# Block maxima on all partitions, mask zeroing on VectorE, and copies dealt anew among three engines

## The chip, the cores and the metric

The kernel runs on one core of one Trainium2 chip. The metric is the device time of one execution in microseconds (us). TensorE (PE) multiplies, VectorE (DVE), ScalarE (ACT) and GpSimd (POOL) work on tiles, SyncE (SP) issues most of the transfers. A profile is one execution of the program, taken by the hardware profiler. PEld are TensorE's weight loads, and a name with a q behind it (SPq) is an engine's queue of issued transfers.

## What is computed

Three layers follow one another: block-causal attention (blocks of 64), a feed-forward layer with a gated convolution over the sequence, and a feed-forward layer with a spatial gate. Cut to what matters:

```python
# attention: q, k, v of 4 x 8 x 576 x 64
scores = np.matmul(q, k.transpose(0, 1, 3, 2)) / np.sqrt(64)
scores = np.where(block_i >= block_j, scores, -1e9)
scores = scores - np.max(scores, axis=-1, keepdims=True)
attn = np.exp(scores)
attn = attn / (np.sum(attn, axis=-1, keepdims=True) + 1e-09)
x = np.matmul(attn, v)                      # then 4 x 576 x 512
# first layer, d_ff = 1024
h = np.maximum(x @ w_in, 0.0)
conv = sum(conv_w[k] * shift(h, k - 1) for k in range(3))
x = (h * sigmoid(conv)) @ w_out
# second layer
h = np.maximum(x @ w_in, 0.0)
u, v = h[..., :512], h[..., 512:]
v_n = (v - mean(v)) / sqrt(var(v) + 1e-6)
out = (u * (w_spatial @ v_n + b_spatial)) @ w_out
```

## The kernel before

The 32 heads are worked off as 16 pairs; a pair's two heads lie on partitions 0 to 63 and 64 to 127. For each pair the program loads keys and queries (`raw`), rounds both (`kp`, `qp`), and TensorE multiplies them once for the maxima alone (steps x0 to x3 of a pair, `tile_max` and `last_max`). VectorE reduces these scores out of PSUM. A 128-query tile holds two blocks of 64: the lower block sees the keys up to its own block, the upper one 64 keys more. So `mx` takes the maximum over what both see, on 128 partitions, and `mxu` the maximum over the 64 further keys, on partitions 64 to 127 only. The last block of 64 queries, whose queries lie in `qlast` for both heads, has 576 keys; when its scores lie in two banks, two reductions go to `mxl` and are joined. `max_up` joins `mx` and `mxu`, and TensorE transposes the result (`max_tr`). The row of maxima then goes by a transfer into the mask operand `mq`, and a product of `mk` and `mq` subtracts the maximum and masks in the score bank itself (line 1028). ACT takes the exponential, TensorE sums with the values, and `norm_a` normalises.

All products of the two layers run on float32 numbers that are split into a rounded high part and the rest, the low part (`h` and `l` in names), three products for each. The weights come as 64-bit words, and `words_to_f32` makes them float32 in steps (a scaled copy on ACT, a sign mask, two shifts); `split64` then makes high and low part. For each of the 64 gate tiles (`in1`), ACT and VectorE make the convolution and the gate, and GpSimd rounds the result into `g` (line 662); the low part is a subtraction on VectorE or GpSimd (`minus`, line 669).

What runs where is fixed by hand-made tables: `SEQ` is the order of TensorE's steps (x, y: maxima; s: scores; v: value sums; m: first layer; p: second layer; f: matmuls that only fill), `ORDER` the order on each other engine, `BIND` which buffer a step takes. Masks of bits (`KL_POOL`, `SGN_POOL`, `Q_DVE` and so on) say which engine has a copy or a low part. `Order` plays the program through with estimated durations and emits the instructions in that order.

At the start GpSimd zeroes `mk` and three `mq`, and issues the transfers of their constant rows (`start`, lines 1312 to 1317); VectorE zeroes the rest (`start2`), and TensorE spins on 16 small products until the first keys land.

## Time and profile before

| what | value |
|---|---|
| median of 3 runs | 606.75 us (605.97 to 607.78) |
| the profiled execution, its own time | 607.56 us |
| its span, first to last instruction | 605.70 us |
| TensorE busy | 576.7 us, 95% |
| VectorE busy | 443.8 us, 73% |
| ACT busy, GpSimd busy | 249.1 us, 214.1 us |
| TensorE's granted clock, mean | 0.985 |

The shares are means over stages that differ. The attention with its preparations fills roughly the first 140 us, then attention and the first layer run beside one another until about 290 us, the first layer ends near 405 us, and the rest is the second layer. An idle time in a row stands in brackets, with what ended it. Busy shares by stretch tell which engine has no time left in a stretch; idle time of TensorE can be read directly as a stretch's length less its busy time.

### The profile page before, as it was taken

How to read it: one execution, taken by the hardware profiler on the slowest of the kernel's cores; microseconds unless marked ns; L12 is line 12 of the kernel's file. 1: busy time of each engine (PE TensorE's matmuls, PEld its weight loads, DVE VectorE, ACT ScalarE, POOL GpSimd, SP SyncE). 2: the span in 40 equal slices, each digit the busy share in tenths (PEclk: the TensorE clock that was granted, in tenths of full speed). 3: DMA queues.
4: the chain of work that ended last, by engine and by line, in shares of the span. 5: the costliest groups of instructions: out<-in, count | busy, mean ns of one | idle time of the engine just before them, and what ended most of it. 6: DMA issues, size and time to landing. Idle time of an engine off the chain costs nothing.

```text
span 605.7 us, 11928 instructions
## 1 busy us (share of the span) xinstructions
PE 576.7 (95%) x4612; PEld 515.0 (85%) x4612; DVE 443.8 (73%) x930; ACT 249.1 (41%) x517; POOL 214.1 (35%) x269
## 2 busy tenths in 40 slices
PE   6888789999999999999999999999999999999997
PEld 4655467879898888889988999999989989998996
DVE  4999989985919786986835489877797474455556
ACT  3565545554346542534525275636063023013101
POOL 5422423536352556446414354643211121121020
PEclk7999989999999999999999999999999999999999
DMA  7554453015132213303012474434713400520012
GB/s 225 183 187 157 152 177 122 0 60 161 43 99 62 89 53 123 101 21 121 1 41 82 122 237 152 136 109 110 227 37 106 137 31 0 163 74 2 22 38 78
DMA packets 43542, 61.22 MB, mean 101 GB/s; under 512 B 8949, under 2 KB 34293, under 8 KB 43486
## 3 DMA queue, kind: packets, MB, share of 16 engines
q1 hardware_dynamic: 43226, 60.37, 31.1%
q8 instruction: 36, 0.59, 0.4%
q0 software_dynamic: 256, 0.09, 0.1%
q14 instruction: 20, 0.16, 0.1%
q10 hardware_dynamic: 4, 0.00, 0.0%
HBM read 46.08 MB, written 14.23 MB: 100 GB/s over the span
## 4 chain that ended last, share of the span: by engine, by line
PE 62%; DVE 12%; ACT 2%; issue 1%; POOL 1%; DVEq 0%; POOLq 0%; ACTq 0%
PE mo L651 41%; PE s L651 11%; PE st L659 3%; DVE cc L1195 3%; PE st L1024 3%; DVE cc L1199 1%; PE st L651 1%; DVE g L665 1%; DVE mx L903 1%; PE st L1028 1%; PE st L1016 1%; PE st L898 1%; DVE w_f L753 1%; DVE x L665 0%; DVE mxu L903 0%
## 5 line engine op out<-in xcount | busy, mean ns | idle before, releaser
L651 PE MATMUL mo<-x,w1i_h 128*128 128x290 f32 x504 | 108.0, 301 | 1.3 <-ACT h L1189 0.7
L651 PE MATMUL mo<-g,w1o_h 128*128 128x288 f32 x464 | 98.1, 298 | 0.5 <-ACT h L1189 0.5
L651 PEld LDWEIGHTS mo<-x,w1i_h 128*128 128x128 f32 x504 | 82.8, 188 | 5.0 <-issue 1.9
L1195 DVE SCALAR_TENSOR_TENSOR cc<-h,cwt,cc 128x288 f32<-128x288 f32 x128 | 71.1, 573 | 21.0 <-ACT cc L1192 20.3
L651 PEld LDWEIGHTS mo<-g,w1o_h 128*128 128x128 f32 x464 | 76.1, 189 | 2.9 <-issue 1.7
L662 POOL TENSOR_SCALAR g<-cc 128x288 fp32r<-128x288 f32 x64 | 38.9, 612 | 105.3 <-DVE cc L1199 97.4
L651 PE MATMUL mo<-x,w1i_l 128*128 128x290 f32 x252 | 75.0, 297 | 0.0
L651 PE MATMUL mo<-g,w1o_l 128*128 128x288 f32 x232 | 68.6, 296 | 0.0
L1037 ACT ACTIVATE e<-st 128x1024 f32<-128x1024 f32 (+1 forms) x64 | 53.1, 836 | 32.3 <-PE st L1028 26.1
L662 POOL TENSOR_SCALAR g<-ga 128x288 fp32r<-128x288 f32 x40 | 19.4, 496 | 100.3 <-DVE ga L1518 54.3
L651 PE MATMUL mo<-x,w2i_h 128*128 128x288 f32 x256 | 51.8, 295 | 0.1
L659 PE MATMUL st<-e,v 128*64 128x448 f32 (+4 forms) x384 | 49.2, 407 | 0.5 <-DVE mt L966 0.5
L651 PEld LDWEIGHTS mo<-x,w1i_l 128*128 128x128 f32 x252 | 47.4, 188 | 0.0
L659 PEld LDWEIGHTS st<-e,v 128*64 128x64 f32 x384 | 26.0, 142 | 24.7 <-issue 18.0
L903 DVE TENSOR_REDUCE mx<-st 128x2 f32<-128x640 f32 (+2 forms) x64 | 42.5, 679 | 6.1 <-PE st L898 5.8
L651 PEld LDWEIGHTS mo<-g,w1o_l 128*128 128x128 f32 x232 | 43.6, 188 | 0.0
L651 PEld LDWEIGHTS mo<-x,w2i_h 128*128 128x128 f32 x256 | 41.2, 188 | 0.5 <-ACT u L1492 0.3
L1192 ACT ACTIVATE cc<-h,cwt 128x288 f32<-128x288 f32 x64 | 33.9, 534 | 15.7 <-DVE g L665 11.0
L651 PE MATMUL s<-w2i_h,x 128*128 128x512 f32 x128 | 39.5, 390 | 0.0
L651 PE MATMUL mo<-ws_h,vnh 128*128 128x288 f32 x135 | 39.4, 296 | 0.0
L1197 ACT ACTIVATE cc<-cc 128x288 f32<-128x288 f32 x64 | 27.8, 439 | 24.3 <-DVE cc L1195 23.9
L651 PE MATMUL mo<-x,w2i_l 128*128 128x288 f32 x128 | 37.7, 294 | 0.0
(186 smaller groups left out, 1408.6 us busy)
## 6 DMA issues: line engine op xcount, KB each, us to landing
x2d<-y SPq DMA_DIRECT2D x32, 288.0 KB
x<-x2d SPq DMA_DIRECT2D x16, 576.0 KB
raw<-in_kq_dram SPq DMA_DIRECT2D x15, 576.0 KB
v<-in_vt_dram SPq DMA_DIRECT2D x16, 320.0 KB
rb<-rd SPq DMA_DIRECT2D x32, 144.0 KB
out_dram<-o SPq DMA_DIRECT2D x32, 144.0 KB
x<-in_w2i_dram SPq DMA_DIRECT2D x8, 512.0 KB
w_raw<-in_w1i_dram SPq DMA_DIRECT2D x4, 512.0 KB
```

The costliest lines, as they stand in the source:

```text
L651: nc.tensor.matmul(o, w, x, start=start, stop=stop)
L659: nc.tensor.matmul(o[row:row + m], w, x, start=start, stop=stop)
L662: nc.gpsimd.tensor_scalar(o, i, 1.0, 0.0, ALU.mult, ALU.add)
L665: nc.vector.tensor_tensor(o, a, b, ALU.subtract)
L753: yield ("DVE", t_dve(n), lambda: nc.vector.scalar_tensor_tensor(f.bitcast(U32), f.bitcast(U32), 3, s, ALU.logical_shift_left, ALU.bitwise ...
L898: nc.tensor.matmul(st[:, e, o:o + n], qp[r, 128 * c:128 * c + 128], kp[r, 0:n], start=True, stop=True)
L903: return ("DVE", t_dve(2 * i.shape[-1] * (i.shape[2] if len(i.shape) == 4 else 1)), lambda: nc.vector.tensor_reduce(o, i, AX.X, ALU.max), ...
L1024: nc.tensor.matmul(st[:, e, o:o + nq], keys(kx, slice(64 * e, 64 * e + 64)), qx[e], start=j == 0, stop=False)
L1037: yield ("ACT", t_act(2 * n), lambda: nc.scalar.activation(ex[:, :, e0:e0 + n], st[:, :, 0:n], ACTF.Exp, scale=0.125), 0, 0)
L1192: yield ("ACT", t_act(HT, False, 1), lambda: nc.scalar.activation(cc, h[:, o:o + HT], ACTF.Copy, scale=cwt[:, c, 1:2]), 0, P_G)
L1195: yield ("DVE", t_dve(HT, ptr=1), lambda: nc.vector.scalar_tensor_tensor(cc, h[:, o + e:o + e + HT], cwt[:, c, j:j + 1], cc, ALU.mult, ALU ...
L1197: yield ("ACT", t_act(HT, False), lambda: nc.scalar.activation(cc, cc, ACTF.Tanh, scale=0.5), 0, P_G)
```

## The change

- The upper maxima `mxu` are reduced on all 128 partitions. On the lower 64 they then hold something that must not count, so `max_up` joins with a limit per partition: minimum with `lim` (-3.0e38 below, 3.0e38 above), then maximum with `mx`, in one scalar_tensor_tensor. The join of the two halves of the last block becomes a reduction over two elements. The small buffers are four deep instead of two.
- VectorE zeroes `mk` and the three `mq`; GpSimd issues only their transfers. All zeroing is emitted ahead of the first load.
- The bit masks are replaced by `ENG`, a table with a letter for each instance (A, D or P). New are the choices for the high parts of weights (`WH`), of `x` (`XH`) and `g` (`GH`), for each key and query copy (`K`, `Q`), each half of `qlast` (`QE`), and each of the four score sums of a pair (`ADD`).
- `SEQ`, `ORDER` and `BIND` are new tables. Among the first transfers, the convolution's taps (`cwr`) and the identity come earlier, and pair 1 is loaded before pair 2. TensorE's sequence has 26 filling products instead of 32 (the 16 of the spin among them).

```diff
-                    yield red(up[64:128].rearrange("p (e c) -> p e c", e=2)[:, :, 0:2],
-                              st.rearrange("p e (i x) -> p e i x", x=256)[64:128, :, :, 64:128])
+                    yield red(up.rearrange("p (e c) -> p e c", e=2)[:, :, 0:2],
+                              st.rearrange("p e (i x) -> p e i x", x=256)[:, :, :, 64:128])
...
-                    yield red(up[64:128, c:8:4], st[64:128, :, 128 * c + 64:128 * c + 128])
+                    yield red(up[:, c:8:4], st[:, :, 128 * c + 64:128 * c + 128])
...
-                    yield ("DVE", 0.08, lambda: nc.vector.tensor_tensor(mx[:, 8:9], two[:, 0:1], two[:, 1:2], ALU.max), 0, 0, True)
+                    yield ("DVE", 0.09, lambda: nc.vector.tensor_reduce(mx[:, 8:9], two, AX.X, ALU.max), 0, 0)
...
-        yield ("DVE", 0.08, lambda: nc.vector.tensor_tensor(mx[64:128, 0:8], mx[64:128, 0:8], up[64:128], ALU.max), 0, 0, True)
+        yield ("DVE", 0.14, lambda: nc.vector.scalar_tensor_tensor(
+            mx[:, 0:8], up, lim, mx[:, 0:8], ALU.min, ALU.max), 0, 0, True)
...
-        yield ("ACT", t_act(512, False), lambda: nc.scalar.activation(hi, fv, ACTF.Copy), 0, prio)
-        yield minus(not (W_DVE >> unit) & 1, lo, fv, raw(hi), 512, prio)
+        yield copies("WH", unit, hi, fv, 512, prio)
+        yield minus("W", unit, lo, fv, raw(hi), 512, prio)
...
-        yield ("POOL", t_round(S), lambda: pool_round(x1[:, 0, :], x), 0, NPR + 1)
-        yield minus((X1_POOL >> p) & 1, x1[:, 1, :], x, raw(x1[:, 0, :]), S, NPR + 1)
+        yield copies("XH", p, x1[:, 0, :], x, S, NPR + 1)
+        yield minus("X", p, x1[:, 1, :], x, raw(x1[:, 0, :]), S, NPR + 1)
...
-                yield ("POOL", t_round(HT), lambda: pool_round(g[:, 0, :], cc), 0, P_G)
-                yield minus((GLO_POOL[2 * b + hf] >> c) & 1, g[:, 1, :], cc, raw(g[:, 0, :]), HT, P_G)
+                yield copies("GH", 16 * b + 8 * hf + c, g[:, 0, :], cc, HT, P_G)
+                yield minus("G", 16 * b + 8 * hf + c, g[:, 1, :], cc, raw(g[:, 0, :]), HT, P_G)
...
     def start():
-        for t, c in [(mk, 0)] + [(t, 1) for t in mq]:
-            nc.gpsimd.memset(raw(t), 0.0)
-            for e in range(2):
-                nc.gpsimd.dma_start(out=t[64 * e:64 * e + 5], in_=kc[c])
-        yield ("POOL", 6.4, None, 0, 0)
+        yield ("POOL", 1.9, consts([(mk, 0)], nc.gpsimd))
+        yield ("mark", ("mk",))
+        yield ("POOL", 3.2, consts([(t, 1) for t in mq], nc.gpsimd))
...
+    def zeros():
         spin(od_mo[0])
         nc.vector.memset(eps, 1e-6)
+        for t in [mk] + mq:
+            nc.vector.memset(raw(t), 0.0)
+        nc.vector.memset(lim[0:64], -3.0e38)
+        nc.vector.memset(lim[64:128], 3.0e38)
...
+ENG = {
...
+    "WH": "PDAPAPPPPAPDPPDPDPDPPDAP",
+    "K": "APPPPDPPPAAAAPPPP",
+    "GH": "PAPAPAPPDAPDPAPADDAPPAAAPDAPAAAPPDPAPAAPAAAADAAPAAPDAPAAAAAPDPAP",
...
+    def copies(table, i, o, x, n, prio):
+        return alt(table, i,
+                   A=on("A", n, lambda: nc.scalar.activation(o, x, ACTF.Copy), prio),
+                   D=on("D", n, lambda: nc.vector.tensor_copy(o, x), prio, fast=True),
+                   P=on("P", n, lambda: pool_round(o, x), prio))
```

Three places show how instructions move. First GpSimd at the start; `mk` and `mq` are the mask operands, `qlast` the last 64 queries of a pair (a number behind a name counts buffers). Before:

```order
L1314 MEMSET mk 128x576
L1316 DMA mk<-in_kc_dram 5x576 x2
L1314 MEMSET mq_147 128x576
L1316 DMA mq_147<-in_kc_dram 5x576 x2
L1314 MEMSET mq_148 128x576
L1316 DMA mq_148<-in_kc_dram 5x576 x2
L1314 MEMSET mq_149 128x576
L1316 DMA mq_149<-in_kc_dram 5x576 x2
L662 ISA
L662 TENSOR_SCALAR qlast_150<-raw 64x64 x2
```

Now:

```order
L1332 DMA mk<-in_kc_dram 5x576 x2
L666 ISA
L666 TENSOR_SCALAR kp_153<-raw 128x320
L1332 DMA mq_148<-in_kc_dram 5x576 x2
L1332 DMA mq_149<-in_kc_dram 5x576 x2
L1332 DMA mq_150<-in_kc_dram 5x576 x2
L666 TENSOR_SCALAR kp_155<-raw 128x576
L666 TENSOR_SCALAR qlast_152<-raw 64x64
```

Pair 0's `qlast` has left this queue (ACT makes it), the second half of pair 0's keys has come into it, and the zeroing is gone.

Second VectorE during the maxima of pair 3, up to the join (L951 before, L969 now). Before:

```order
L903 TENSOR_REDUCE mxu<-st_111 64x2
L903 TENSOR_REDUCE mx<-st_110 128x2
L941 TENSOR_TENSOR mx<-mxl 128x1
L749 TENSOR_SCALAR x_448<-x_448 128x512
L903 TENSOR_REDUCE mxu<-st_110 64x2x2
L903 TENSOR_REDUCE mx<-st_110 128x2
L751 SCALAR_TENSOR_TENSOR x_448<-x_448 128x512
L824 CAST qp_153<-raw 128x576
L903 TENSOR_REDUCE mxu<-st_110 64x2
L1157 TENSOR_TENSOR xp_130<-xp_130,rb 128x160
L951 TENSOR_TENSOR mx<-mx,mxu 64x8
L753 SCALAR_TENSOR_TENSOR w_f_138<-w_f_138,x_448 128x512
```

Now:

```order
L921 TENSOR_REDUCE mxu<-st_112 128x2
L778 SCALAR_TENSOR_TENSOR x_428<-x_428 128x512
L921 TENSOR_REDUCE mxu<-st_111 128x2x2
L1136 COPY xp_132<-st_113 128x576
L921 TENSOR_REDUCE mx<-st_111 128x2
L921 TENSOR_REDUCE mxu<-st_111 128x2
L959 TENSOR_REDUCE mx<-mxl 128x1
L1173 TENSOR_TENSOR xp_131<-xp_131,rb 128x160
L969 SCALAR_TENSOR_TENSOR mx<-mxu,lim,mx 128x8
L1173 TENSOR_TENSOR xp_131<-xp_131,rb 128x288
L780 SCALAR_TENSOR_TENSOR w_f_139<-w_f_139,x_428 128x512
```

The upper maxima and the join now have 128 partitions, and the join of the last block has one operand; the sign mask (L749) and a query copy (L824) are not in this piece any more.

Third VectorE at the very end, where `g` rows are low parts for the last products of the second layer and `y` and `o` rows add products up. Before:

```order
L1597 TENSOR_TENSOR y_135<-y_135,mo_109 128x288
L1597 TENSOR_TENSOR y_135<-y_135,mo_108 128x288
L1597 TENSOR_TENSOR o_4551<-y_135,mo_108 128x288
L1597 TENSOR_TENSOR o_4552<-y_135,mo_109 128x288
L1597 TENSOR_TENSOR y_136<-y_136,s_3850 128x288
L1597 TENSOR_TENSOR y_136<-y_136,s_3852 128x288
L665 TENSOR_TENSOR g_123<-ga_4559,g_123 128x288
L1597 TENSOR_TENSOR o_4549<-y_136,s_3852 128x288
```

Now:

```order
L1627 TENSOR_TENSOR y_137<-y_137,s_3851 128x288
L669 TENSOR_TENSOR g_117<-ga_4544,g_117 128x288
L1627 TENSOR_TENSOR y_136<-y_136,mo_110 128x288
L1627 TENSOR_TENSOR y_136<-y_136,mo_109 128x288
L1627 TENSOR_TENSOR o_4536<-y_136,mo_109 128x288
L1627 TENSOR_TENSOR o_4537<-y_136,mo_110 128x288
L1627 TENSOR_TENSOR y_137<-y_137,s_3847 128x288
L1627 TENSOR_TENSOR y_137<-y_137,s_3849 128x288
```

The last low part stood behind six additions, and now stands ahead of them.

## Rows read from the trace of the kernel before

**Rows 1.** Table of stretches: length, each engine's busy time (instructions), granted clock, DMA.

```profile
11.15:138.37 127.22, 109.72 (x1079) 82.94 (x1079) 116.19 (x236) 71.37 (x134) 43.80 (x47) 0.95 0.39 130
138.37:590.00 451.63, 448.99 (x3425) 416.26 (x3423) 310.83 (x647) 172.87 (x375) 160.99 (x200) 1.00 0.29 91
590.00:605.70 15.70, 11.56 (x83) 10.88 (x81) 11.01 (x27) 1.93 (x5) 1.47 (x3) 0.98 0.22 75
```

**Rows 2.** Waits of TensorE from 0 to 150 us: total, times, longest.

```profile
PE st L959 <- DVE mx L951: 3.9, 5, 1.6
PE st L898 <- DVE mxu L903: 3.0, 4, 1.5
```

**Rows 3.** Timeline of VectorE: start, duration (us), engine, line, operation, tiles.

```profile
29.04 0.45 DVE L1129 TENSOR_SCALAR srow<-st 128x288 f32<-128x288 f32 x1
29.41 1.08 DVE L903 TENSOR_REDUCE mx<-st 128x2 f32<-128x896 f32 x1
...
30.85 0.69 DVE L751 SCALAR_TENSOR_TENSOR x<-x 128x512 uint32<-128x512 uint32 x1
31.58 0.30 DVE L903 TENSOR_REDUCE mxu<-st 64x2 f32<-64x128 f32 x1
31.91 0.96 DVE L753 SCALAR_TENSOR_TENSOR w_f<-w_f,x 128x512 uint32<-128x512 uint32 x1
```

**Rows 4.** VectorE's groups by shape (busy us, mean ns | idle before), then one line's instructions.

```profile
L749 DVE TENSOR_SCALAR x<-x 128x512 uint32<-128x512 uint32 x13 | 7.1, 547 | 1.3 <-ACT w_f L741 1.3
L665 DVE TENSOR_TENSOR w1i_l<-w_f,w1i_h 128x512 fp32r<-128x512 f32 x4 | 3.4, 860 | 0.1
L824 DVE CAST qp<-raw 128x576 fp32r<-128x576 f32 x6 | 3.0, 501 | 5.6 <-DMA raw<-in_kq_dram 5.6
L941 DVE TENSOR_TENSOR mx<-mxl 128x1 f32<-128x1 f32 x8 | 2.9, 363 | 0.1
L1676 DVE MEMSET ws_l<- 33x576 f32 x1 | 0.5, 538 | 0.2 <-DVE vnl L665 0.2
...
L941 DVE TENSOR_TENSOR mx<-mxl x8: 145/156/1197, 11.0 to 90.9; 128x1 f32<-128x1 f32 x8
```

**Rows 5.** Timeline: GpSimd's instructions beside VectorE's.

```profile
31.66 1.57 POOL L747 TENSOR_SCALAR w_raw<-w_raw 128x512 f32<-128x512 f32 x1 [2.55 <-ACT w_f L741]
...
69.00 1.40 POOL L669 TENSOR_TENSOR raw<-raw,kp 128x576 fp32r<-128x576 f32 x1 [5.12 <-PE st L1028]
69.02 1.41 DVE L951 TENSOR_TENSOR mx<-mx,mxu 64x8 f32<-64x8 f32 x1
...
70.45 1.86 DVE L665 TENSOR_TENSOR w1o_l<-w_f,w1o_h 128x512 fp32r<-128x512 f32 x1
```

**Rows 6.** Timeline of the start, first keys to first mask product.

```profile
4.09 0.32 DVE L824 CAST qp<-raw 128x256 fp32r<-128x256 f32 x1 [2.37 <-DMA raw<-in_kq_dram]
4.19 1.15 SPq L1347 DMA_DIRECT2D cwr<-in_cw_dram  x1
...
9.48 0.85 PE L651 MATMUL mo<-kp,qlast 128*128 128x288 f32 x2 [2.24 <-POOL qlast L662]
...
11.15 0.17 DVE L951 TENSOR_TENSOR mx<-mx,mxu 64x8 f32<-64x8 f32 x1
...
11.93 0.37 PE L959 MATMUL st<-ident,mx 128*9 128x128 f32 x1 [1.60 <-DMA ident<-in_cst_dram]
...
15.59 0.76 PE L1028 MATMUL st<-mq,mk 64*128 64x320 f32 x4
```

**Rows 7.** Timeline of the last matmuls.

```profile
600.68 0.54 PE L651 MATMUL mo<-g,w2o_h 128*128 128x288 f32 x2 [0.31 <-DVE g L665]
```

**Rows 8.** Table of stretches between joins, and the end of the first layer.

```profile
57.35:69.02 11.67, 10.43 (x115) 6.91 (x115) 11.36 (x25) 7.10 (x12) 2.09 (x5) 1.00 0.60 199
69.02:85.33 16.31, 11.57 (x107) 7.38 (x109) 13.25 (x23) 5.22 (x11) 4.81 (x4) 0.79 0.38 131
100.20:124.20 24.00, 22.80 (x169) 20.47 (x171) 23.35 (x49) 14.13 (x32) 10.71 (x14) 1.00 0.08 27
360.00:400.00 40.00, 39.45 (x279) 38.25 (x278) 36.05 (x67) 22.72 (x50) 21.71 (x23) 1.00 0.39 124
```

More of the change, by code (lines that the diff above doesn't have):

```diff
@@ L767, in split64 @@
         f = yield ("take", "wf")
-        yield from words_to_f32(r, f, r[:, :, 1], prio, "ACT" if (SGN_ACT >> unit) & 1 else "POOL" if (SGN_POOL >> unit) & 1 else "DVE")
+        yield from words_to_f32(r, f, r[:, :, 1], prio, unit)
         yield ("free", home, n)
@@ L791, in load_pairs @@
     def load_pairs():
+        yield ("wait", ("head",))
         for p in range(NPAIR):
@@ L831, in one @@
             yield ("mark", key)
-        second = dve if p == 0 or (Q_DVE >> p) & 1 else act if (Q_ACT >> p) & 1 else pool
         for i, c in enumerate(parts):
@@ L836, in prep_pair @@
             n = c.stop - c.start
-            od.spawn(one(act(kp[:, c], t[:, 0, c], n), ("kpq", p, i, 0)), "att", 0.0, f"one{p}{i}0")
-            od.spawn(one(second(qp[:, c], t[:, 1, c], n), ("kpq", p, i, 1)), "att", 0.0, f"one{p}{i}1")
+            od.spawn(one(copies("K", p if i == 0 else 16, kp[:, c], t[:, 0, c], n, P_KPQ), ("kpq", p, i, 0)), "att", 0.0, f"one{p}{i}0")
+            od.spawn(one(copies("Q", p if i == 0 else 16, qp[:, c], t[:, 1, c], n, P_KPQ), ("kpq", p, i, 1)), "att", 0.0, f"one{p}{i}1")
         def ends():
@@ L842, in ends @@
                 r = slice(64 * e, 64 * e + 64)
-                yield (act if (QL_ACT >> p) & 1 else pool)(ql8[r, r], t[r, 1, 512:S], 64)
+                yield copies("QE", 2 * p + e, ql8[r, r], t[r, 1, 512:S], 64, P_KPQ)
             yield ("mark", ("ql8", p))
@@ L861, in load_vs @@
     def load_vs():
-        yield ("sleep", 0.06)
+        yield ("wait", ("head",))
         for p in range(NPAIR):
@@ L935, in task @@
                 else:
-                    two = att.tile([128, 2], F32, name="mxl", tag="mxl", bufs=2)
+                    two = att.tile([128, 2], F32, name="mxl", tag="mxl", bufs=4)
                     for i in range(2):
@@ L1060, in score @@
         if part == 1:
-            return dict(needs=[("m", p)], rings=[], fn=fn, tile=True)
+            return dict(needs=[("m", p), ("mk",)], rings=[], fn=fn, tile=True)
         return dict(needs=[("m", p)] + ([] if f32_scores(p) else [("kl", p)]), rings=[("st", 1)] + ([(f"e{g}", 1)] if i == 0 else []), fn=fn,
@@ L1309, in attn_moe_moe2_kernel, with consts, ld @@
     od.pick = pick
-    def start():
-        for t, c in [(mk, 0)] + [(t, 1) for t in mq]:
-            nc.gpsimd.memset(raw(t), 0.0)
-            for e in range(2):
-                nc.gpsimd.dma_start(out=t[64 * e:64 * e + 5], in_=kc[c])
-        yield ("POOL", 6.4, None, 0, 0)
+    def consts(tiles, q):
+        def ld():
+            for t, c in tiles:
+                for e in range(2):
+                    q.dma_start(out=t[64 * e:64 * e + 5], in_=kc[c])
+        return ld
+    def start():
+        yield ("POOL", 1.9, consts([(mk, 0)], nc.gpsimd))
+        yield ("mark", ("mk",))
+        yield ("POOL", 3.2, consts([(t, 1) for t in mq], nc.gpsimd))
     def spin(o):
@@ L1343, in start2 @@
             nc.vector.memset(raw(t), 0.0)
-        yield ("sleep", 1.0)
+        for h in HBUF:
+            nc.vector.memset(h[:, 0:292:291], 0.0)
+    def start2():
+        yield ("wait", ("head",))
         def ld():
             nc.sync.dma_start(out=cwr, in_=words(cw))
-        for h in HBUF:
-            nc.vector.memset(h[:, 0:292:291], 0.0)
         yield from dma(od, 25000, ld, 0)
-        yield ("sleep", 10.0)
         yield from words_to_f32(cwr, cwt.rearrange("p c t -> p (c t)"), cwr[:, :, 1], CWP)
@@ L1354, in later @@
     def later(t, gen, key):
-        yield ("sleep", t)
+        yield ("wait", ("head",))
         yield from gen
@@ L1367, in prep_all_w1 @@
     def prep_all_w1():
+        yield ("wait", ("head",))
         yield ("sleep", PREP_AT)
@@ L1690, in w2o_f32 @@
         f = W2F[k] = yield ("take", "wf")
-        yield from words_to_f32(r, f, r[:, :, 1], 1, "ACT" if (SGN_ACT >> 24 + k) & 1 else "DVE")
+        yield from words_to_f32(r, f, r[:, :, 1], 1)
         yield ("free", "wr", slot)
```

139 lines of the change are left out of this document (71 added, 68 removed), and 258 rows, old and new, of tables (BIND, ORDER).

## The prediction, made before the changed kernel ran

> **What bounds the kernel now.** I read the table of stretches first, then the waits of TensorE, then single rows.
>
> [rows 1] cut the span into four. From 138 us on TensorE is busy 449.0 of 451.6 us: nothing that another engine does there can win more than 2.6 us. The loss lies in the 127.2 us between the first pair's joined maximum (11.15) and the tenth's (138.37): TensorE is idle 17.5 us, and its granted clock is 0.95. VectorE is busy 116.2 us there, 91%, more than TensorE's 86%; ACT and GpSimd have half their time free. So in that window VectorE sets the pace, and TensorE waits for what VectorE does last for a pair: [rows 2], the joined maxima (3.9 us) and the upper maxima that free a score bank (3.0 us). Before 11.15 the start chain counts, after 590 the tail.
>
> **The change part by part.**
>
> *Upper maxima on 128 partitions.* The same 128 or 256 elements per partition are reduced, so the reduction itself costs what it did. What changes is the seam between neighbours. In [rows 3] the row copy at 29.04 takes 0.45 us, yet the next reduction starts at 29.41, 0.08 us before it ends. The upper maximum at 31.58 starts 0.04 after the row ahead of it ends (30.85 + 0.69), and its other neighbour starts at 31.91, 0.03 after its own end. Over all rows without an idle time, ordinary neighbours overlap by 0.08 us (median of 573), and a seam with an upper maximum or a join on one side gaps by 0.02 to 0.03 us (39 into an upper maximum, 30 out of one; one of each kind stands in the group). That is 0.10 us a seam. The order of VectorE has 62 such seams between the first and the tenth join, and after the change none: 62 x 0.10 = **6.2 us** of VectorE's time. Bounds: 0, if the gap comes from something else than the start at partition 64; 6.8, with 0.11.
> The rows don't say whether the half count of partitions or the start makes the gap. [...]
>
> *The join of the last block.* The 128x1 tensor_tensor becomes a reduction of one operand. The eight took 2.9 us [rows 4]; the shortest took 0.145, the median 0.156, the longest 1.197. Seven lie in the window, all but the first, undisturbed one: 2.75 us. As reductions at 0.15 us they are 1.05: **-1.7 us** (bounds -0.6, with the 0.30 of an upper maximum for each, and -2.0). The 128x8 join with the limit stays one instruction of two operands: nothing, within 0.1 us for all sixteen.
>
> *Copies and low parts on other engines.* Counted in the orders up to the tenth join, at [rows 4]: six sign masks leave VectorE, 6 x 0.55 = -3.3. Four high-part copies come, 4 x 0.50 = +2.0. Low parts: w1o four more, w1i one fewer, 3 x 0.86 = +2.6. Two more low parts of g, 288 of the 512 columns of w1i's and so 2 x 0.48 = +1.0. The small rest (a key low part, three 64x64 copies and a row copy against an x low part, an evacuation and one gate step) nets under 0.5. Sum **+2.3 us**; bounds 0 and +3.5, as several of these means hold waits that need not recur. What VectorE gains after the tenth join, about 26 us by the same durations, lies where it is busy 311 of 452 us [rows 1]: taken as nothing, covered by TensorE's own work; without that cover it is rival 3.
>
> *GpSimd beside VectorE.* At 69.00 a two-operand instruction of GpSimd starts, and the 0.17 us join of pair 5 takes 1.41 us; the next one stretches w1o's low part to 1.86 us [rows 5]. A one-operand instruction does less: beside the sign step at 31.66 VectorE's row at 31.91 takes 0.96 us, against 0.69 for the same shape at 30.85. Up to the first score sum, GpSimd loses 7 of its 18 two-operand instructions and gains about 14 one-operand ones (8 key copies, 10 weight copies, 6 sign steps, less g and x copies). At 0.27 each that is +3.8 us, and 7 two-operand ones that each held VectorE for 0 to 1.2 us give back 0 to 8. I take **0**, bounds +4 and -4.
> [...]
>
> So VectorE needs 6.2 + 1.7 - 2.3 = **5.6 us** less in the window. VectorE is busy 91% of it, so I let 0.9 through to TensorE: **-5.0 us**. The rest waits on exponentials, copies and transfers that don't change.
>
> *The start.* [rows 6]: the first cast waits 2.37 us for its data, until 4.09. The four zeroings that move to VectorE cost 0.54 us each by the 33x576 memset [rows 4], with two tiny ones 2.3 us: hidden under that wait with 0.1 to spare; were each 0.1 longer, the cast would come 0.3 late. GpSimd is then free of them, and ACT makes the 64x64 ends, so TensorE no longer waits 2.24 us for GpSimd's at 9.48; the last block of pair 0 comes about 1.5 us earlier. But it is not last: the joined maximum at 11.15 stands at the end of VectorE's reductions, and the second half of pair 0 is now issued behind the taps' load (1.15 us of SP's queue), so the second tile starts some 0.5 us later. The join comes at about 11.2, as before. The identity, which held the transposition until 11.93 (1.60 us), is now issued ahead of pair 2's load and of the first values, behind which it stood. The transposition so starts at about 11.4: **-0.5 us** on the first mask rows at 15.59 (bounds +0.5, if the later half costs more, and -1.5).
>
> *The tail.* In the order of before six additions stand on VectorE ahead of the last low part, and TensorE stands 0.31 us for it at 600.68 [rows 7]. Now all low parts stand ahead of these additions: **-0.3 us** (0 to -0.5).
>
> Sum: -5.0 - 0.5 - 0.3 = -5.8 us. The profiled execution took 607.56 us (span 605.70, and 1.86 around it), 0.81 above the median of the runs: 607.56 - 0.81 - 5.8 = **600.95 us**.
>
> **The rivals.**
>
> [...] GpSimd's busy time in the window was 43.8 us [rows 1]; the 24 one-operand instructions that come, priced at 0.27 us of VectorE's time each without credit for what leaves, cost 6.5 us and eat the 5.6. For it: the sign steps among them are 1.57 us long, as the one at 31.66. Against it: the worst rows were two-operand ones [rows 5]. Start and tail remain: 606.75 - 0.8 = 605.95.
> [...]
> The same time comes out if the seams stay, because the reductions wait for one another anyway.
>
> *Rival 3: VectorE overfull, slower.* Between the eighth and the ninth join VectorE is busy 23.35 of 24.00 us, and TensorE 22.80 [rows 8]. The order puts 6.1 us more of VectorE's work there (27.8 for 21.7 by the same durations), less 0.6 for six seams: 5.5, or 4.9 beyond its idle 0.65. The next stretch has 4.1 us less, but TensorE could win back only its 1.4 idle us there: +3.5. Again from 360 to 400, VectorE is busy 36.05 of 40 and gets 5.2 more: +1.3. It decides if the relief of the first eight pairs doesn't pass, since TensorE waits there for other things: 606.75 + 4.8 - 0.8 = 610.75. Against it: the work there is early weight work, which can slip.
>
> *Rival 4: more than the seams.* From the sixth to the seventh join [rows 8], 16.31 us pass, at a granted clock of 0.79, against 11.67 for the stretch before, with as many matmuls (107 and 115). It began with the stalled join and low part of [rows 5]: TensorE stood still, and then ran its sums at the lower level. If that pair of stalls goes, some 3 us more are saved than I count: 598.0. Against it: other stalls may fall elsewhere.
>
> **How the numbers follow.** Forecast 0.56, its own range 597.5 to 604.5; rival 2 0.22; rival 3 0.12; rival 4 0.10. About 0.3%, 1.8 us, is what a measurement can tell from no change: below 604.9 is faster, above 608.6 slower. Faster: 0.95 of the forecast, rival 4, a quarter of rival 2: 0.53 + 0.10 + 0.06 = 0.69. Same: the rest of these two, 0.03 + 0.16 = 0.19. Slower: 0.12. The predicted time is the forecast's. The range leaves out rival 3 and the far end of rival 4: 596.5 to 608.0.
>
> **What would show it.** Right: around the upper maxima VectorE's rows overlap by 0.08 us; the tenth join comes at 132 to 134 instead of 138.37; TensorE's idle time from the first to the tenth join falls from 17.5 to about 12.5; the mask rows of pair 0 start near 15.1; no wait of TensorE in the last 6 us. Wrong: seams unchanged at +0.03; rows of VectorE over 1 us beside GpSimd's copies (rival 2); the stretch up to the ninth join longer than 24 us, or TensorE idle between 360 and 400 (rival 3); a granted clock below 0.9 in a stretch where it was 1.00.

## The result, and the profile after

The changed kernel takes 596.91 us (median of four runs, 595.44 to 597.73), the kernel before 606.87 in the same comparison (605.97 to 607.78). The ratio is 0.9833, 95% interval 0.9807 to 0.9859: 10 us faster, where the forecast was 600.95 and a gain of 5.8. The profiled execution took 597.48 us.

The page of the changed kernel, its span, the busy times and the granted clock in 40 slices:

```profile
span 595.4 us, 11879 instructions
...
PE 576.0 (97%) x4606; PEld 514.9 (86%) x4606; DVE 448.4 (75%) x985; ACT 247.6 (42%) x527; POOL 166.0 (28%) x206
...
PEclk9999999999999999999999999999999999999999
```

The table of stretches that answers to [rows 1]: from the first to the tenth joined maximum, up to the tail, and the tail (length, busy times of the engines, granted clock, DMA):

```profile
11.42:128.26 116.84, 107.51 (x1075) 82.32 (x1075) 108.84 (x240) 63.35 (x115) 52.05 (x54) 1.00 0.44 141
128.26:580.00 451.74, 449.04 (x3424) 415.86 (x3421) 320.73 (x691) 178.62 (x399) 106.52 (x134) 1.00 0.28 90
580.00:595.40 15.40, 11.67 (x85) 11.16 (x84) 11.50 (x29) 2.10 (x6) 1.53 (x3) 1.00 0.25 88
```

All of the gain lies in the first line: 127.22 us became 116.84. TensorE's idle time there fell from 17.5 to 9.3 us, and its busy time from 109.7 to 107.5 at nearly the same work (1075 products instead of 1079), with the granted clock at 1.00 instead of 0.95. VectorE still is the busiest engine of the window, 93%. The first join comes 0.27 us later than before, and what follows the tenth join takes 467.14 us instead of 467.33.

The stretches that answer to [rows 8], from the fifth to the seventh join, from the eighth to the tenth, and the end of the first layer:

```profile
54.73:66.17 11.44, 10.82 (x137) 7.84 (x135) 10.79 (x27) 7.05 (x10) 6.00 (x6) 1.00 0.55 173
66.17:76.42 10.25, 8.86 (x111) 6.13 (x109) 10.22 (x22) 6.15 (x11) 6.56 (x6) 1.00 0.69 218
...
90.35:118.54 28.19, 26.28 (x204) 22.43 (x207) 27.18 (x60) 16.89 (x39) 10.50 (x13) 1.00 0.24 87
118.54:128.26 9.72, 9.08 (x105) 7.89 (x97) 8.10 (x20) 4.56 (x11) 2.21 (x2) 1.00 0.02 5
...
360.00:400.00 40.00, 39.73 (x255) 37.09 (x254) 32.59 (x67) 18.75 (x40) 13.74 (x15) 1.00 0.42 130
```

One stretch alone, from the sixth to the seventh join, gives 6.1 of the 10.4 us: 16.31 at a clock of 0.79 became 10.25 at 1.00.

TensorE's waits up to 150 us that answer to [rows 2] (total, times, longest), with the longest new one at the head:

```profile
PE st L916 <- ACT qp L685: 2.0, 1, 2.0
PE st L978 <- DVE mx L969: 1.9, 3, 0.9
PE st L916 <- DVE mxu L921: 1.4, 1, 1.4
```

VectorE's timeline around an upper maximum of the changed kernel (start, duration), which answers to [rows 3]:

```profile
69.87 0.75 DVE L921 TENSOR_REDUCE mx<-st 128x2 f32<-128x640 f32 x1
70.55 0.27 DVE L921 TENSOR_REDUCE mxu<-st 128x2 f32<-128x128 f32 x1
70.74 0.31 DVE L1173 TENSOR_TENSOR xp<-xp,rb 128x160 f32<-128x160 f32 x1
```

The upper maximum starts 0.07 us before its neighbour ends (69.87 + 0.75), and the next row 0.08 before its own end. Over all rows without an idle time the median is -0.08 us for 43 seams into an upper maximum and for 31 out of one. Where the join directly follows an upper maximum, whose result it reads, a gap of 0.035 us stays, as before.

The trace of the kernel before has seven more seams that bear on this: those between two upper maxima, which both lie on partitions 64 to 127. All seven overlap by 0.08 us. In this row two of them, 0.30 and 0.29 us long, take 0.50 together:

```profile
118.90 0.50 DVE L903 TENSOR_REDUCE mxu<-st 64x2 f32<-64x128 f32 x2
```

So a start at partition 64 makes no gap by itself; the gap stands where a row on 64 to 127 meets one that starts at 0.

### The profile page after: what moved, and what is told of

Its sections match the earlier page's. It is cut to its first block, busy times and chain, and to the rows that moved or that the text cites. A ratio compares the mean times of both kernels' runs of the same rounds, so it can differ in the third digit from the quotient of the medians.

```text
span 595.4 us, 11879 instructions
## 1 busy us (share of the span) xinstructions
PE 576.0 (97%) x4606; PEld 514.9 (86%) x4606; DVE 448.4 (75%) x985; ACT 247.6 (42%) x527; POOL 166.0 (28%) x206
## 4 chain that ended last, share of the span: by engine, by line
PE 70%; DVE 15%; POOL 4%; ACT 3%; issue 3%; DMA 2%; SPq 0%; DVEq 0%; ACTq 0%; POOLq 0%
PE mo L655 42%; PE s L655 9%; PE st L663 7%; PE st L1042 4%; PE st L1034 2%; PE st L916 2%; DVE cc L1211 2%; PE st L1046 2%; DVE mx L921 1%; DVE w_f L780 1%; DVE g L669 1%; PE st L655 1%; POOL g L666 1%; DMA w_raw<-in_w2o_dram 1%; DMA raw<-in_kq_dram 1%
## 5 line engine op out<-in xcount | busy, mean ns | idle before, releaser
L1211 DVE SCALAR_TENSOR_TENSOR cc<-h,cwt,cc 128x288 f32<-128x288 f32 x128 | 67.1, 539 | 7.6 <-ACT cc L1208 6.6
L1055 ACT ACTIVATE e<-st 128x1024 f32<-128x1024 f32 (+2 forms) x64 | 52.9, 836 | 26.4 <-PE st L1046 24.9
L921 DVE TENSOR_REDUCE mx<-st 128x2 f32<-128x128 f32 (+2 forms) x64 | 42.4, 680 | 8.5 <-PE st L916 8.5
L666 POOL TENSOR_SCALAR g<-cc 128x288 fp32r<-128x288 f32 x23 | 14.9, 651 | 115.8 <-DVE cc L1215 113.0
L663 PE MATMUL st<-e,v 128*64 128x448 f32 (+4 forms) x384 | 46.7, 392 | 0.1
L1046 PE MATMUL st<-mq,mk 64*128 64x320 f32 (+1 forms) x192 | 37.9, 394 | 0.0
```

The source lines that it names most:

```text
L663: nc.tensor.matmul(o[row:row + m], w, x, start=start, stop=stop)
L666: nc.gpsimd.tensor_scalar(o, i, 1.0, 0.0, ALU.mult, ALU.add)
L921: return ("DVE", t_dve(2 * i.shape[-1] * (i.shape[2] if len(i.shape) == 4 else 1)), lambda: nc.vector.tensor_reduce(o, i, AX.X, ALU.max), ...
L1046: nc.tensor.matmul(st[:, e, o:o + nq], keys(mk, r), q[r, q0:q0 + nq], start=False, stop=True)
L1055: yield ("ACT", t_act(2 * n), lambda: nc.scalar.activation(ex[:, :, e0:e0 + n], st[:, :, 0:n], ACTF.Exp, scale=0.125), 0, 0)
L1211: yield ("DVE", t_dve(HT, ptr=1), lambda: nc.vector.scalar_tensor_tensor(cc, h[:, o + e:o + e + HT], cwt[:, c, j:j + 1], cc, ALU.mult, ALU ...
```

## Experiments

All ratios are against the kernel before, in runs on the same chip; intervals are 95%. The second time of the 128 partitions, the filling steps and the last row were measured on another chip than the other experiments; the kernel before takes 607.80 us there, and 607.2 beside the others. Ratios compare better than medians.

| kernel | median us | ratio | interval |
|---|---|---|---|
| the changed kernel | 596.91 | 0.9833 | 0.9807 to 0.9859 |
| before, 128 partitions (first, second time) | 595.09, 594.18 | 0.9798, 0.9777 | 0.9783 to 0.9813, 0.9763 to 0.9790 |
| before, reduction for the last block's join | 606.96 | 0.9993 | 0.9982 to 1.0004 |
| changed, upper maxima on 64 to 127 | 602.77 | 0.9926 | 0.9913 to 0.9938 |
| before, upper maxima on 0 to 63 | 593.35 | 0.9774 | 0.9757 to 0.9791 |
| before, pair 5's low parts on VectorE | 605.17 | 0.9961 | 0.9946 to 0.9976 |
| before, all edits of the maxima | 594.66 | 0.9785 | 0.9762 to 0.9807 |
| changed, second half ahead of the taps | 595.52 | 0.9805 | 0.9783 to 0.9827 |
| before, 128 partitions, filling steps | 594.79 | 0.9785 | 0.9771 to 0.9798 |
| before, 128 partitions, two moves at the start | 592.62 | 0.9760 | 0.9740 to 0.9780 |
| the same with four edits more | 592.44 | 0.9749 | 0.9734 to 0.9764 |

Where the time lies, from the profiled execution of each (us, joins counted from the first):

| kernel | to join 1 | 1 to 6 | 6 to 7 | 7 to 8 | 8 to 10 | after 10 |
|---|---|---|---|---|---|---|
| before | 11.15 | 57.87 | 16.31 | 14.87 | 38.17 | 467.3 |
| changed | 11.42 | 54.75 | 10.25 | 13.93 | 37.91 | 467.1 |
| before, 128 partitions, first time | 10.95 | 52.74 | 10.43 | 17.52 | 36.27 | 466.3 |
| the same, second time | 11.11 | 52.69 | 10.43 | 14.78 | 37.11 | 466.0 |
| changed, upper maxima on 64 to 127 | 11.45 | 55.56 | 12.21 | 16.16 | 38.69 | 466.6 |
| before, pair 5's low parts on VectorE | 11.23 | 59.36 | 12.31 | 15.55 | 38.17 | 467.4 |
| before, reduction for the last block's join | 11.22 | 56.50 | 14.90 | 14.85 | 38.96 | 467.5 |
| before, 128 partitions, two moves at the start | 10.95 | 52.42 | 10.79 | 14.39 | 36.35 | 466.0 |
| the same with four edits more | 9.84 | 53.42 | 10.43 | 14.74 | 37.11 | 466.1 |

### The seams alone, and the change without them

The kernel before with the 128 partitions and the limit (tables kept):

```diff
-                    yield red(up[64:128, c:8:4], st[64:128, :, 128 * c + 64:128 * c + 128])
+                    yield red(up[:, c:8:4], st[:, :, 128 * c + 64:128 * c + 128])
...
-        yield ("DVE", 0.08, lambda: nc.vector.tensor_tensor(mx[64:128, 0:8], mx[64:128, 0:8], up[64:128], ALU.max), 0, 0, True)
+        yield ("DVE", 0.14, lambda: nc.vector.scalar_tensor_tensor(
+            mx[:, 0:8], up, lim, mx[:, 0:8], ALU.min, ALU.max), 0, 0, True)
```

> The kernel before, its tables and engines kept; only the upper maxima are reduced on 128 partitions and joined with the limit. Theory (seams): VectorE's rows around the upper maxima overlap by 0.08 us instead of standing 0.03 apart, VectorE needs about 6 us less between the first and the tenth join, 127.2 us become about 122, and the time falls by 5 to 6 us to about 601.5. Rival (tables): the seams close, but in the old order TensorE waits for other things, and the time stays within 1.8 us of 606.9. Beside both: if the fall of the granted clock in the stretch after the sixth join (0.79) hangs on where pair 5's low parts on GpSimd meet the join, a shift of a few tenths can end it, worth 3 to 6 us by itself; the clock of that stretch tells which part of a gain is that.

The changed kernel with the same lines taken the other way:

> The changed kernel with the upper maxima and their join back on partitions 64 to 127; everything else of the change is kept. Theory (seams): about 60 seams of 0.10 us come back before the tenth join, and the time rises by 5 to 6 us to about 602.5. Rival (tables): the new order hides them, the time stays within 1.8 us of 596.9.

Measured: 595.09 us and 602.77. In the changed kernel the seams are worth 5.9 us, as expected; between the runs whose granted clock was 1.00 throughout it is nearly the same, 602.15 against a median of 596.34. In the order of before the 128 partitions are worth 12.1, twice the expectation. This kernel is no slower than the whole change: the interval of its first run touches that of the changed kernel, the second lies below it. So the 128 partitions alone bring all of the gain, and with them in place the rest of the change wins nothing and probably costs 2 to 3 us. Without them, the rest of the change wins 4.4 us. Its trace is 4.1 us shorter from the sixth to the seventh join (16.31 to 12.21) and 2.3 from the first to the sixth, and 1.8 longer from the seventh to the tenth. From the sixth to the seventh join the two edits are not additive: alone they save 5.9 and 4.1 us there, together 6.1, so both remove the same thing.

What that is, the second trace of the kernel with 128 partitions shows: VectorE's timeline around pair 5's join.

```profile
63.20 0.68 DVE L752 SCALAR_TENSOR_TENSOR x<-x 128x512 uint32<-128x512 uint32 x1
63.80 0.22 DVE L952 SCALAR_TENSOR_TENSOR mx<-mxu,lim,mx 128x8 f32<-128x8 f32 x1
63.94 0.68 DVE L665 TENSOR_TENSOR w1o_l<-w_f,w1o_h 128x512 fp32r<-128x512 f32 x1
...
65.51 1.17 DVE L1159 TENSOR_TENSOR xp<-xp,rb 128x160 f32<-128x160 f32 x1
```

And GpSimd's, in the same trace:

```profile
64.53 1.96 POOL L669 TENSOR_TENSOR raw<-raw,kp 128x576 fp32r<-128x576 f32 x1 [4.41 <-PE st L1030]
66.45 1.50 POOL L669 TENSOR_TENSOR raw<-raw,qp 128x576 fp32r<-128x576 f32 x1
```

In [rows 5] GpSimd's instruction began 0.02 us ahead of the join, which then took 1.41 us. Here VectorE comes to the join 0.73 us ahead of GpSimd, and the join takes 0.22. The instruction of GpSimd waits for TensorE's score products (L1030), and VectorE has come that much further by then. A stall is still there, 1.17 us at 65.51, but on a row that TensorE doesn't wait for at once: the reduction into `mxl` (65.14), for which TensorE waits next, already lies ahead of it.

In the changed kernel the new tables have moved these pieces too: VectorE makes pair 5's key low part there, and GpSimd's one instruction for pair 5 begins 0.52 us behind the join.

```profile
66.17 0.21 DVE L969 SCALAR_TENSOR_TENSOR mx<-mxu,lim,mx 128x8 f32<-128x8 f32 x1
66.92 1.90 DVE L669 TENSOR_TENSOR w1o_l<-w_f,w1o_h 128x512 fp32r<-128x512 f32 x1
```

A stall is left here too (1.90 us), again on a row that TensorE doesn't wait for at once.

### The reduction in the last block's join

```diff
-                    yield ("DVE", 0.08, lambda: nc.vector.tensor_tensor(mx[:, 8:9], two[:, 0:1], two[:, 1:2], ALU.max), 0, 0, True)
+                    yield ("DVE", 0.09, lambda: nc.vector.tensor_reduce(mx[:, 8:9], two, AX.X, ALU.max), 0, 0)
```

> The kernel before, its tables and engines kept; only the join of the last block's two halves is a reduction of one operand instead of a tensor_tensor. Theory: the eight joins fall from 2.9 us in all (one of 1.2) to about 1.1, seven of them in the window, and the time falls by 1.5 us (605.4). Rival: the stall of 1.2 us moves on to the next two-operand row beside the same GpSimd instruction, and the time stays within 0.5 us of 606.9.

Measured: 606.96 us against 607.19, no difference. All eight of these joins now take 0.14 or 0.15 us. VectorE's timeline of this kernel, where the join of 1.197 us in [rows 4] was:

```profile
37.29 0.14 DVE L941 TENSOR_REDUCE mx<-mxl 128x1 f32<-128x2 f32 x1
37.35 1.41 DVE L749 TENSOR_SCALAR x<-x 128x512 uint32<-128x512 uint32 x1
```

GpSimd beside it:

```profile
37.20 1.27 POOL L669 TENSOR_TENSOR w1i_l<-w_f,w1i_h 128x512 fp32r<-128x512 f32 x1 [5.08 <-ACT w1i_h L772]
```

The rival holds: the stall of a microsecond moves to the row behind, the sign mask, which takes 1.41 us instead of the 0.42 of an undisturbed one.

The same trace has a second lesson, at pair 5's join. VectorE comes to it 0.02 us ahead of GpSimd here, where it came 0.02 us behind in [rows 5]:

```profile
67.73 0.16 DVE L951 TENSOR_TENSOR mx<-mx,mxu 64x8 f32<-64x8 f32 x1
67.92 1.80 DVE L665 TENSOR_TENSOR w1o_l<-w_f,w1o_h 128x512 fp32r<-128x512 f32 x1
69.64 1.88 DVE L753 SCALAR_TENSOR_TENSOR w_f<-w_f,x 128x512 uint32<-128x512 uint32 x1
...
67.75 1.42 POOL L669 TENSOR_TENSOR raw<-raw,kp 128x576 fp32r<-128x576 f32 x1 [5.12 <-PE st L1028]
...
72.07 0.76 PE L1330 MATMUL mo<-full 64*128 64x222 f32 x4 [3.15 <-DVE mxl L938]
```

The join is undisturbed, 0.16 us, but both stalls move to the two rows behind it. These still stand ahead of the reduction into `mxl`, so TensorE now waits 3.15 us for that one. The stretch takes 14.90 us, at a granted clock of 0.89, and the time of the kernel is unchanged. So a shift of some hundredths that frees the join doesn't end the collision; VectorE has to be past the rows that TensorE waits for.

### The start or the count of partitions

```diff
-                    yield red(up[64:128, c:8:4], st[64:128, :, 128 * c + 64:128 * c + 128])
+                    yield red(up[0:64, c:8:4], st[0:64, :, 128 * c + 64:128 * c + 128])
```

> The kernel before with the upper maxima and their join on partitions 0 to 63 instead of 64 to 127: half the partitions, but starting at 0. The maxima are so taken over other keys than they should; nothing else changes. Theory (the start in another quadrant makes the gap): VectorE's rows around the upper maxima overlap by 0.08 us, and the time is that of the kernel with 128 partitions. Rival (the half count makes it): the rows stand 0.03 us apart as before, and the time stays within 1.8 us of 606.9.

Measured: 593.35 us. VectorE's timeline around an upper maximum on partitions 0 to 63:

```profile
72.54 0.75 DVE L665 TENSOR_TENSOR x<-xp,x 128x576 fp32r<-128x576 f32 x1
73.21 0.28 DVE L903 TENSOR_REDUCE mxu<-st 64x2 f32<-64x128 f32 x1
73.41 0.67 DVE L751 SCALAR_TENSOR_TENSOR x<-x 128x512 uint32<-128x512 uint32 x1
```

Both seams overlap by 0.08 us, with 64 partitions beside 128. The time is that of the second run of the 128 partitions (ratios 0.9774 and 0.9777). So the count of partitions doesn't matter; with the seven seams between upper maxima (above), it is the change of the start between neighbours, from partition 0 to 64 or back, that makes the gap of 0.01 to 0.03 us.

### Pair 5's collision alone

```diff
-KL_POOL = 0x71f5
-QL_POOL = 0xa879
+KL_POOL = 0x71d5
+QL_POOL = 0xa859
...
-max_up5 split64.9 split64.10 x30
+max_up5 split64.9 prep_pair50*2 split64.10 x30
```

> The kernel before, but pair 5's two low parts of keys and queries are made by VectorE, behind its joined maximum and w1o's low part, and no longer by GpSimd beside them. Seams and all other tables as before. Theory (a single collision costs more than its stalls): the join of pair 5 takes 0.17 us instead of 1.41 and the low part behind it 0.7 instead of 1.86; VectorE does 1.5 us more work there; the stretch from the sixth to the seventh join falls from 16.3 to about 12.5 us at a granted clock of 1.00, and the time falls by 3 to 4 us to about 603.5. Rival (the seams set the pace there too): the stretch loses under 1 us, and the time stays within 1.8 us of 607.2.

Measured: 605.17 us, 2.0 less, half of what was expected. The stretch from the sixth to the seventh join and the next one:

```profile
70.59:82.90 12.31, 8.95 (x115) 6.49 (x115) 12.07 (x25) 6.71 (x12) 2.05 (x2) 0.99 0.57 183
82.90:98.45 15.55, 15.33 (x136) 12.60 (x137) 14.29 (x30) 9.11 (x18) 6.22 (x5) 0.79 0.52 171
```

VectorE's timeline at the join:

```profile
70.59 0.16 DVE L951 TENSOR_TENSOR mx<-mx,mxu 64x8 f32<-64x8 f32 x1
70.78 0.69 DVE L665 TENSOR_TENSOR w1o_l<-w_f,w1o_h 128x512 fp32r<-128x512 f32 x1
71.39 0.75 DVE L665 TENSOR_TENSOR raw<-raw,kp 128x576 fp32r<-128x576 f32 x1
```

The join takes 0.16 us and the low part 0.69, and the stretch falls by 4.0 us, although VectorE has 1.5 us more to do in it. So the collision's price in its own stretch is shown, with the seams still there: 4.0 us, or up to 5.5 if that work were free. Part of it is TensorE's clock: the sums over the values take 5.39 us in the trace of before, where the granted clock was 0.50 from 72.7 to 79.6 us, and 2.92 here and in the changed kernel.

TensorE's timeline, the first three rows before, the last in this kernel:

```profile
70.48 0.28 PE L959 MATMUL st<-ident,mx 128*9 128x128 f32 x1 [1.64 <-DVE mx L951]
...
73.46 0.77 PE L1330 MATMUL mo<-full 64*128 64x222 f32 x4 [2.02 <-DVE mxl L938]
...
74.51 5.39 PE L659 MATMUL st<-e,v 128*64 128x128 f32 x24
...
72.11 2.92 PE L659 MATMUL st<-e,v 128*64 128x128 f32 x24
```

What took part of it back in this trace lies elsewhere: the granted clock fell one stretch later (0.79, 15.55 us against 14.87), and the identity landed later than in the trace of before (TensorE waited 2.8 us for it instead of the 1.60 of [rows 6]).

### All that is done to the maxima

> The kernel before with all that the change does to the maxima (128 partitions, the limit, the last block's join as a reduction, small buffers four deep), and none of its tables, engines or zeroing. Theory (the seams were all of it, and the rest of the change costs): within 0.6 us of 595.1, the time with the 128 partitions alone, and so below the changed kernel's 596.9. Rival (the tables bring part of the gain only beside the reduction or the deeper buffers): above 596.

Its edit is the two diffs above together, and bufs=4 instead of 2 for the three small tiles. Measured: 594.66 us, as the theory expects. The reduction and the deeper buffers add nothing that can be measured to the 128 partitions.

### The start of the changed kernel

```diff
-        "first first_load0 start2 first_load1 prep_pair11
+        "first first_load0 first_load1 start2 prep_pair11
...
-        "one000 start2 ends0 one011 ends0 split64 x4*2 split64.2
+        "one000 one011 ends0*2 split64 x4*2 start2 split64.2
```

(On VectorE the taps' two first steps moved behind the second pair's maxima; on ACT pair 0's query copy now stands ahead of its `qlast` copies.)

> The changed kernel with pair 0's second half loaded ahead of the convolution's taps, its query copy ahead of the qlast copies on ACT, and the taps' conversion later on ACT and VectorE. Theory (the taps' load ahead of the second half is what the start lost): TensorE's wait of 2.0 us for pair 0's query copy falls under 0.8, the second join comes at about 21 instead of 22.18, and the time falls by 1 to 1.5 us to about 595.6. Rival (VectorE sets the second join): the wait goes, the second join stays within 0.4 us of 22.18, and the time within 0.6 us of 596.9.

Measured: 595.52 us, 1.4 less than the changed kernel; the intervals of the two overlap, but the trace shows where it comes from. TensorE's wait of 2.0 us is gone, the first join comes at 9.92 instead of 11.42, the second at 20.68, and from the fourth on all come 1.6 us earlier. TensorE's timeline of the changed kernel shows what the second half of pair 0, issued 0.6 us later behind the taps in SP's queue, had done:

```profile
7.69 1.12 PE L916 MATMUL st<-kp,qp 64*128 64x384 f32 x4 [2.04 <-ACT qp L685]
...
11.69 0.38 PE L978 MATMUL st<-ident,mx 128*9 128x128 f32 x1 [0.74 <-DVE mx L969]
...
15.50 0.72 PE L1046 MATMUL st<-mq,mk 64*128 64x320 f32 x4
```

### The clock's fall

The first trace of the 128 partitions has a fall of the clock, from the seventh to the eighth join. Filling steps of TensorE were put in just ahead of it (three `f` in `SEQ`), and beside that kernel the unfilled one was profiled a second time.

> The kernel before with the upper maxima on 128 partitions, and three filling steps of TensorE around pair 7's qlast product, where TensorE stood 0.43 and 0.38 us before its granted clock fell to one half from 76.6 to 83. Nothing that they compute is used. Theory (the fall is what that idle time costs, and it costs 2 to 3 us): the granted clock stays at 1.00 from the seventh to the eighth join, that stretch takes 14.4 to 15 us instead of 17.5, and the time falls by 1.5 to 2.5 us to about 593. Rival (VectorE sets that stretch, and the clock only follows): the clock may stay up, the stretch stays above 16.5, the time within 0.6 us of 595.1.

> The kernel before with the upper maxima on 128 partitions once more, as a second trace of the same program beside the one with filling steps. Theory (the fall comes from this order): the granted clock falls between the seventh and the eighth join again, and that stretch takes about 17.5 us. Rival (the fall comes by chance from run to run): it stays at 1.00, the stretch takes about 15 us, and the time is nearer to 593.5 than to 595.1.

The stretch in the first trace of the unfilled kernel:

```profile
74.12:91.64 17.52, 16.71 (x149) 13.47 (x146) 14.48 (x31) 10.91 (x22) 5.69 (x5) 0.81 0.50 160
```

In its second trace:

```profile
74.23:89.01 14.78, 13.92 (x151) 11.20 (x147) 13.85 (x31) 10.63 (x21) 5.54 (x5) 1.00 0.54 187
```

And with the filling steps:

```profile
75.11:89.85 14.74, 14.54 (x157) 11.88 (x153) 13.75 (x32) 10.60 (x21) 5.73 (x5) 1.00 0.58 192
```

The theory that this order brings the fall is wrong: the same program runs once with it and once without, and the filling steps have nothing to show (594.79 us where 593 was expected). The two traces come from two chips, but one chip does both as well: the first four runs of this program, on one chip, have mean clocks from 0.987 to 1.000. The fall cost 2.7 us in its stretch (17.52 against 14.78), and the two profiled executions differ by 2.05 us (595.97 and 593.92). In whole times its price is smaller and not settled: the run at 1.000 took 594.98 us, the one at 0.993 took 594.14. Of 38 runs of the kernel before beside these experiments, the 16 with a mean clock of 0.993 or more have a median of 607.3 us, the 13 with 0.987 or less 607.9. So the gain of 10 us is not one of clock alone.

### A version that beats both

Two moves of the change at the start, on the kernel before with 128 partitions: ACT makes pair 0's `qlast`, and the identity is loaded ahead of pair 2.

```diff
-QL_ACT = 0x419c
+QL_ACT = 0x419d
...
-        "first_load0 first_load1 first prep_pair22 prep_pair11 load_vs later start2
+        "first_load0 first_load1 first later prep_pair22 prep_pair11 load_vs start2
```

> The kernel before with the upper maxima on 128 partitions, and in addition two of the change's moves at the start: the identity is loaded ahead of pair 2, and ACT makes pair 0's qlast. Theory (the start term of the prediction was right in kind): TensorE's waits for qlast (2.1 and 0.9 us) and for the identity (1.7 us) go, the first mask rows come about 1 us earlier, and the time falls by 0.5 to 1.5 us below the 595.1 of the 128 partitions alone. Rival (the start is hidden by VectorE's maxima of the next pairs): the first mask rows come earlier, the third join doesn't, and the time stays within 0.5 us of 595.1.

Then with the score products of pair 0 behind its maxima (SEQ begins xxxys instead of xsxxy), VectorE's reductions reordered to it, pair 1 loaded first, and the reduction in the last block's join:

> The kernel before with the upper maxima on 128 partitions, the last block's join as a reduction, ACT making pair 0's qlast, and the start in the order that the changed kernel has: pair 0's score products behind its maxima, pair 1 and the identity loaded ahead of pair 2. All other tables and engines of before. Theory (the start counts one for one, as in the run with the taps' load moved): the first join comes at 10.0 instead of 10.95, the later ones about 1 us earlier too, and the time falls 1 us below the 592.6 of the run without the moved score products. Rival (the start is hidden): the first join comes earlier, the sixth doesn't, and the time stays within 0.5 us of 592.6.

Measured: 592.62 and 592.44 us, 4 us below the changed kernel. In the first, the waits for pair 0's `qlast` and for the identity are gone, and in their place TensorE waits 2.17 us for the join itself, which stays at 10.95. The first mask rows, expected 1 us earlier, come at 15.17 (15.06 and 15.47 without the two moves). Its third join comes 0.4 us earlier, and its interval overlaps that of the second run without the two moves: a gain of 1 to 2 us is likely, but not settled, and where it comes from is open. In the second the first join comes at 9.84, and the sixth at 63.26 against 63.37, as the rival says, but not for its reason. VectorE stands idle for pair 1's products, and TensorE for pair 1's rounded keys. ACT makes these behind pair 2's `qlast`, and waits 1.45 us for pair 2's data, which are loaded behind pair 1 in this kernel:

```profile
12.32 0.82 PE L651 MATMUL mo<-kp,qlast 128*128 128x288 f32 x2 [1.81 <-ACT kp L822]
...
10.96 0.52 ACT L822 ACTIVATE qlast<-raw 64x64 fp32r<-64x64 f32 x2 [1.45 <-DMA raw<-in_kq_dram]
11.49 0.68 ACT L822 ACTIVATE kp<-raw 128x576 fp32r<-128x576 f32 x1
```

This product started at 12.16 in the first of the two. The granted clock also fell from 7.9 to 18.1 us in this trace (0.61 from the first to the second join), and not in the other (1.00); how much of the lost microsecond is that, is not separated. The two kernels are the same in time.

## Why the prediction was right, and where its sizes were off

**What bounds it.** Right: only the window from the first to the tenth join changed, and VectorE's relief moved its end. From the tenth join on, 0.2 us changed. Of the signs named, the tenth join came at 128.26 (132 to 134 were expected) and TensorE's idle time fell to 9.3 us (12.5). Both went the way that was forecast, and further: 596.91 us lie below the forecast's own range of 597.5 to 604.5, beyond rival 4's 598.0, and only 0.4 above the end of the widest range.

**Seams, -6.2 us.** Right in cause and in size. These gaps became overlaps (0.08 us in the median), but for the four joins that directly follow an upper maximum, and taking them back in the changed kernel costs 5.9 us. The doubt that the prediction left open, start or count, is settled: it is the change of start, between partitions 0 and 64. The prediction says that the rows don't tell; the seven seams between two upper maxima, with 64 partitions on both sides and an overlap of 0.08 us, had already spoken against the count. The run on partitions 0 to 63 agrees (-0.08 us at 64 partitions).

**Join of the last block, -1.7 us.** Wrong. The joins did fall to 0.14 or 0.15 us, but the kernel with this edit alone takes the same time. The longest join was a stall beside GpSimd, and the stall went to the row behind (1.41 us). The prediction had counted the stall with the operation on which it was seen.

**Copies and low parts, +2.3 us.** Right in sign: VectorE is busy 108.84 us in the window of the changed kernel, and 107.70 in that of the kernel before with all edits of the maxima: +1.1, inside the bounds of 0 and 3.5. What VectorE gains after the tenth join was taken as nothing. It is nearly that: 467.1 us, against 467.3 before, and 466.0, 466.3 and (with the filling steps) 466.9 in the order of before with the 128 partitions. At most 1 us is lost there.

**GpSimd beside VectorE, 0.** Right. If each row of VectorE in the window is set against the lower quartile of its line and shape in the same trace, the excess sums to 12.9 us before, to 8.9 in the changed kernel, and to 9.8 in the second trace with 128 partitions, where GpSimd's work is that of before. In the changed kernel the rows beside two-operand instructions of GpSimd lost 3.3 us (6.0 in that second trace), those beside one-operand ones 5.2 (3.6). So the new choice of GpSimd's operations gave on one side nearly what it took on the other; rival 2, by which GpSimd's one-operand instructions cost VectorE all that it wins, fell.

**0.9 let through, -5.0 us.** This is the term that was mis-sized. Outside the stretch from the sixth to the seventh join, the window lost 4.3 us, near the forecast. In that stretch it lost 6.1, and the prediction had put it into rival 4, at some 3 us and a chance of 0.10. [rows 5] show the join beginning 0.02 us after GpSimd's instruction, and the seams were to make VectorE faster by several tenths in each pair; that made an end of the stall likelier than 0.10. A shift of hundredths would not have done it, as the run with the reduction shows. The price of 16.31 us against 10.3 has three parts: the eight seams of the stretch, 0.8 us by the prediction's 0.10 each; the sums over the values at a granted clock of 0.50, 5.39 us instead of 2.92; and TensorE's standing for the stalled rows (1.64 and 2.02 us before), which makes up about the rest. The granted clock had fallen at 72.7 us, after TensorE had been busy 1.0 of the 3.9 us ahead of that.

**The start, -0.5 us.** Wrong. The identity held nothing up any more, as predicted, but the mask rows came at 15.50 instead of 15.59, the first join 0.27 us later, and the second 1.3 us later. The prediction saw that the second half of pair 0 stood behind the taps' load and took 0.5 us for it; it was 1.5 at the first join, as the run with the loads exchanged shows (together with the new place of the query copy).

**The tail, -0.3 us.** Right: the wait of [rows 7] has no counterpart in the last 6 us, and TensorE's idle time in the stretch of the tail fell from 4.1 to 3.7 us.

**Rival 3.** The stretch from the eighth to the ninth join is longer by 4.2 us, as it said, but 35 more matmuls lie in it, and the next one is 4.5 us shorter. From 360 to 400 us TensorE is idle 0.27 us, less than before. VectorE was nearly full up to the ninth join, 27.18 of 28.19 us, but the two stretches together take 37.91 us instead of 38.17, so nothing was lost by it.

So the way and the cause were right, and the size came out as near as it did partly by luck, through errors that offset each other: 2.0 us were counted that didn't come (nine tenths of the last block's 1.7, and the start's 0.5), and a collision that cost some 5 us beyond the seams of its stretch (6.1 less 0.8) was left to a rival. What the new tables cost beyond the start (0.9805 with it mended, against 0.9785 for the maxima alone) is inside the intervals, and stays open.

## What to carry to other kernels

An instruction of VectorE on partitions 64 to 127 between neighbours that start at 0 cost a tenth of a microsecond on each side here (a gap of 0.01 to 0.03 us instead of an overlap of 0.08); with 62 such seams before the tenth join on the engine that set the pace, computing on all partitions and masking with a limit was cheaper than computing on the upper half, by 12.1 us in the order of before and by 5.9 in that of the changed kernel. Where a trace shows one long stall, look at which rows stand between it and the next one that TensorE waits for: a stall that only moves to the row behind saves nothing (606.96 us against 607.19 in the run with the reduction), while one that moved past that row was not paid by TensorE at once (a row of 1.17 us in the second trace with 128 partitions, in a stretch of 10.43 us instead of 16.31). A new order that comes together with such an edit has to be timed without it and the edit without the order, since each can take the credit for the same stall (5.9 and 4.1 us alone from the sixth to the seventh join, 6.1 together).
